# Value products of the segments' last tokens: one block of 32 tokens at each segment border, in place of a batched stage

## The chip, the core and the metric

The kernel runs on one core of a Trainium2 chip. The core has a matrix engine (PE, with its weight loads shown apart as PEld), a vector engine (DVE), a scalar engine (ACT), a general engine (POOL, which also issues DMAs) and a queue engine (SP, which issues most DMAs). The metric is the device time of one execution in microseconds. Before the change it is 3259.57 us, the median of three runs that lie between 3258.48 and 3265.56 us.

## What is computed

Four layers run one after the other, A B A B, on 2048 tokens of 640 values. Layers A hold nine tenths of the time. A layer A goes through 64 segments of 32 tokens, and each segment needs the one before it: the first 8 rows of a segment's result are the memory that stands ahead of the next segment's 32 tokens.

```python
for s in range(n_seg):
    h = concat([mem, x[:, 32*s : 32*s+32]])          # 8 + 32 rows
    q, k, v = h @ Wq, h @ Wk, h @ Wv                 # 32 heads of 192
    p = softmax(mask(q @ k.T * scale))
    o = (p @ v) @ Wo
    mem = o[:8]                                      # for the next segment
    outs.append(o[8:])
```

Of the 40 rows of `h`, 32 depend on `mem` or stand with it in one block (the 8 memory rows and the first 24 tokens). The last 8 tokens of each segment depend on no other segment in their q, k and v. Those eight are "the segment's last tokens" from here on. Layer B is a linear attention over all tokens, and the change does not touch it.

## The kernel before

**Stages.** The program runs, in each of the two layers A, first a batched stage (`A_pre`), which makes q, k and v of the last tokens of all 64 segments, and then the chain (`A_chain`), which goes through the segments in order. In the profiled execution the first layer's batched stage runs from the start to about 171 us and its chain to about 1370 us; the second layer's batched stage runs from 1643 to 1804 us and its chain to about 3000 us. The two layers B lie behind the two chains.

**The batched stage.** It has 8 steps: two halves of 32 segments by four rounds of 8 heads. A step makes K and Q of its 256 tokens (line 960, 120 matmuls), then V (line 989, 40 matmuls of 128x384). PSUM banks are emptied by DVE and ACT in turn (lines 97 and 99). K and Q go to DRAM as `kqb` (line 974), V goes to DRAM as `vb` (line 997, 64 DMAs of 97 KB a layer, issued by POOL). In the first layer the empty places between these copies are also used for the layer norm of all rows (`all_rows`: POOL loads a block of rows and stores the normalized block), and SP copies the output weights Wo from DRAM to DRAM into another order (`lay_out_wo`, line 792, all four rounds). `early_wo` and `late_wo` bring Wo into SBUF (line 751).

**The chain.** A segment has four rounds n = 0 to 3 of 8 heads each. Per round PE makes Q, K and V of the 32 rows (line 1092, 20 matmuls of 128x384 each, in four column groups of 32), then scores (line 1129), and P times V (line 1142); the products with Wo follow as filling between them (line 1198). ACT brings each PSUM bank to SBUF (lines 1107, 1119, 1172), DVE transposes it (lines 1112, 1285, 1293) or copies half of V (line 1121). For the last tokens POOL loads `kqb` (line 1062) and `vb` (`extra_v`, line 1073: 16 rows of 1552 bytes into rows 64 to 79 of `Vp`) and copies K and Q into place (line 1069).

**The border between two segments.** After the last product with Wo, DVE transposes the result (line 1371) and adds its two halves into the first 8 columns of `hT` (line 1373); PE can then start Q of the next segment. The other 24 columns of `hT` come from the next segment's own tokens: POOL loads them into the tile `xr` (`load_rows`, line 1040), and DVE transposes `xr` into `hT` (`hx_transpose`, line 1043) just ahead of the reciprocals of round 3 (line 1166). `load_rows` is called at the end of a segment for the segment after the next, so that the load has a whole segment's time before it is read. While DVE works at the border, PE runs four idle products of 128x512 (`keep_busy`, line 1205). ACT then copies half of the result (line 1051) and a tail (line 1183); DVE writes the rows to be stored into `orow` (line 1054), and POOL stores them (line 1058).

**Order.** In the chain the order on every engine is written out by hand: each engine goes through its instructions in the order of the program, and a waiting instruction holds up all behind it. SP streams seven pieces of 384 KB of Wq, Wk, Wv and four of 320 KB of Wo in each segment (lines 725 and 774); each is released by a matmul of the round. Each DMA of SP also waits until the eighth DMA before it has landed.

Of the kernel before, what the change touches and what calls it, by code (L numbers as in the profile page):

```python
# [8 lines left out]
P = 128  # L9
# [116 lines left out]
class Kernel:  # L126
# [114 lines left out]
    def rows_of(self, s):  # L241
        return self.xn_rows[32 * s:32 * s + 32, :].rearrange("t (q f) -> q t f", q=4)

# [435 lines left out]
    def layer_A(self, xn_dram, at_dram, li, x_raw=None):  # L679
# [6 lines left out]
        self.vb_d = dram.tile([NSEG, NR, 2, 8, 4 * VH], BF16, name=f"vb{li}")  # L686
# [55 lines left out]
        def load_wo(r, part):  # L742
            for k in part:
# [7 lines left out]
                nc.sync.dma_start(out=into, in_=self.wo_rows[r, :, 1280 * k:1280 * k + 1280])  # L751
# [21 lines left out]
        def load_piece(into, r, c):  # L773
            self.last_load = nc.sync.dma_start(out=into[:, c:c + 1280], in_=self.wo_rows[r, :, own + c:own + c + 1280])
            return self.last_load
# [10 lines left out]
        if li == 0:  # L786
            self.wo_rows = dram.tile([4, P, 7680], BF16, name="wo_rows")

        def lay_out_wo(r):
            for h in range(4):  # L790
                for G in range(2):
                    nc.sync.dma_start(out=self.wo_rows[r, 32 * h:32 * h + 32, 3840 * G:3840 * G + 3840]
                                      .rearrange("f (j m) -> f j m", m=640), in_=wov[8 * r + 4 * G + h])
# [17 lines left out]
    def A_pre(self, xn_dram, li, load_matrix, piece, wo_mid, wo_end, lay_out_wo, early_wo, x_raw):  # L811
# [11 lines left out]
        vts = [wo_end[:, 8 * VH * i:8 * VH * i + 8 * VH].rearrange("p (g f) -> p g f", f=2 * VH) for i in range(2)]  # L823
        with ExitStack() as es:
# [73 lines left out]
            def all_rows():  # L898
# [4 lines left out]
                return [f for i in range(0, len(t), 2) for f in (*t[i:i + 2], None)]  # L903

            for vt in vts:
                nc.vector.memset(vt, 1.0)
            if x_raw is not None:
                first = [norm_tasks(lambda x, k=k: gather(x, x_raw, 0, k, (nc.sync, nc.scalar)),
                                    lambda xn, k=k: normed.__setitem__((0, k), xn)) for k in range(NT)]
                for step in zip(*first):  # L910
                    for f in step:
                        f()
                warm = ps_.tile([P, 512], F32, name="ps_warm", tag="bank")

                def busy(n):
                    for _ in range(n):
                        nc.tensor.matmul(warm[:, :], lhsT=self.ident[:, :], rhs=vts[0].rearrange("p g f -> p (g f)")[:, 0:512],
# [3 lines left out]
            turn = nv = 0  # L921
# [5 lines left out]
            for h, ri, r in steps:  # L927
# [20 lines left out]
                if x_raw is not None and (h, ri) == (NH - 1, 0):  # L948
                    tasks += all_rows()
                if x_raw is not None and h == NH - 1 and ri == NR - 1:  # L950
# [17 lines left out]
                load_matrix("V", r)  # L968
# [6 lines left out]
                if x_raw is not None:  # L975
# [3 lines left out]
                    if h == NH - 1 and ri in (1, 2):  # L979
                        for r1 in (2 * ri - 2, 2 * ri - 1):  # L980
                            lay_out_wo(r1)
                w = [piece("V", r, b) for b in range(KC)]
                for k in range(NT):
                    vt = vts[nv % 2]
                    nv += 1
                    for g in range(4):
                        ps = ps_.tile([P, 512], F32, name="ps_pre", tag="bank")
                        for b in range(KC):
                            nc.tensor.matmul(ps[:, 0:384], lhsT=xBT[:, b, P * k:P * k + P],  # L989
                                             rhs=w[b][:, 384 * g:384 * g + 384], start=(b == 0), stop=(b == KC - 1))  # L990
                        evict(out=self.two_heads(vt[:, g, :]), in_=ps[:, 0:384].rearrange("p (e f) -> p e f", e=2))
                    if x_raw is not None and (h, ri, k) == (0, 0, 0):
# [3 lines left out]
                    for t2 in range(TP):  # L996
                        nc.gpsimd.dma_start(out=self.vb_d[SH * h:SH * h + SH, r, :, TP * k + t2, :],
                                            in_=vt[SH * t2:SH * t2 + SH, :, :].rearrange("p (g x) f -> p g (x f)", x=2))
# [4 lines left out]
    def A_chain(self, xn_dram, at_dram, li, load_slot, piece, late_wo, load_both, wo, low):  # L1003
# [3 lines left out]
        with tc.tile_pool(name=f"A{li}_ch", reuse_waits="tile", bufs=1) as sp, \  # L1007
# [9 lines left out]
            xr = sp.tile([P, 160], BF16, name="xr")  # L1017
            orow = self.under[:, self.ot_at + 768:self.ot_at + 928]
            nc.vector.memset(xr[:], 0.0)
            ots = [self.under[:, self.ot_at + 384 * i:self.ot_at + 384 * i + 384] for i in range(2)]  # L1020
            hT = sp.tile([P, KC, 32], BF16, name="hT", tag="hT")
# [17 lines left out]
            def load_rows(s):  # L1039
                nc.gpsimd.dma_start(out=xr[:], in_=self.rows_of(s))  # L1040

            def hx_transpose(hT, xr=xr):
                nc.vector.transpose(out=hT[:], in_=xr[:].rearrange("p (j b) -> p b j", b=KC))
# [27 lines left out]
            def extra_v(s, n):  # L1071
                r = rounds(s)[n]
                nc.gpsimd.dma_start(out=Vs[n % 2][64:80, :], in_=self.vb_d[s, r].rearrange("g t f -> (g t) f"))  # L1073
# [129 lines left out]
            def keep_busy(ps, w):  # L1203

                nc.tensor.matmul(ps[0:32, 0:w], lhsT=self.ident[:, 0:32], rhs=wo[1, 0][:, 0:w], start=True, stop=True,
                                 tile_position=(0, 0), skip_group_check=True)

# [5 lines left out]
            def weigh(E_before=None):  # L1213
# [5 lines left out]
                return E  # L1219

# [21 lines left out]
            for s in range(NSEG):  # L1242
# [18 lines left out]
                if s > 0:  # L1261
# [40 lines left out]
                for n in range(L):  # L1302
# [36 lines left out]
                    turn(n, osc)  # L1339
                    v_rows(pv, n + 1, "sv")  # L1340
# [128 lines left out]
```

## Time and profile before

| | |
|---|---|
| median of the runs shown | 3259.57 us |
| span of the profiled execution | 3253.7 us |
| PE busy | 3095.3 us, 95% of the span |
| DVE, ACT, POOL busy | 2208.8, 1883.0, 1410.7 us |
| batched stage, first layer (0 to 172 us) | PE 166.3 us busy, DMA share 0.93 |
| batched stage, second layer (1643 to 1810 us) | PE 163.8 us busy, DMA share 0.69 |
| a segment of the chain, border to border | median 18.39 us, mean 18.53 us, 124 of them |
| granted TensorE clock | 1.00 in both stages' windows and in the chain |

The profile is of one execution. Its span is 5.9 us under the median of the runs; no other time is given for the profiled execution, and what lies around its span is taken to be that difference. A group of instructions is shown with the tile that it writes, the tiles that it reads, its count, its busy time, the mean time of one, and the idle time of its engine just before it. Matmuls overlap in the array, so 20 of them with a mean of 0.33 us take 1.0 us together, and the busy time is what to add up.

### The profile page before, as it was taken

The numbers are of one execution on the slowest core, as the hardware profiler recorded it, in microseconds if no ns is written. First come the engines' busy times: TensorE is split into PE (matmuls) and PEld (weight loads), VectorE is DVE, ScalarE is ACT, GpSimd is POOL, SyncE is SP. The second block draws the span as 40 slices with busy tenths as digits, with TensorE's granted clock in tenths as the row PEclk, the third lists the DMA queues.
The fourth block names the chain that finished last, engine by engine and source line by source line (L and its number), as shares of the span: only waits on it lengthen the run. The fifth ranks groups of instructions, "written<-read, shape, count | busy, mean of one in ns | idle before, by whom it ended". The sixth has DMA issues, their size and how long they took to land.

```text
span 3253.7 us, 140890 instructions
## 1 busy us (share of the span) xinstructions
PE 3095.3 (95%) x59424; PEld 1980.2 (61%) x59730; DVE 2208.8 (68%) x5457; ACT 1883.0 (58%) x4481; POOL 1410.7 (43%) x2920
## 2 busy tenths in 40 slices
PE   9989999999999999999999899999999999999999
PEld 7756666666666666555367566666666666665553
DVE  5557777777777777666643577777777777776465
ACT  3346666666666666646433466666666666666453
POOL 3345555555455455430122355555555554554300
PEclk9999999999999999999999999999999999999999
DMA  8977777777777777840385677777777777778400
GB/s 306 372 271 253 256 248 257 232 255 253 236 256 245 244 257 238 285 166 1 113 319 193 240 233 257 248 252 256 242 264 240 259 244 245 255 236 282 149 1 33
DMA packets 325018, 747.58 MB, mean 230 GB/s; under 512 B 65818, under 2 KB 100274, under 8 KB 321314
## 3 DMA queue, kind: packets, MB, share of 16 engines
q1 hardware_dynamic: 254850, 638.55, 56.1%
q0 software_dynamic: 67616, 86.77, 9.7%
q10 hardware_dynamic: 1920, 13.24, 1.0%
q8 instruction: 469, 7.68, 1.0%
q14 instruction: 163, 1.34, 0.1%
HBM read 668.80 MB, written 77.03 MB: 229 GB/s over the span
## 4 chain that ended last, share of the span: by engine, by line
PE 75%; DMA 11%; DVE 8%; issue 3%; ACT 3%; POOL 0%; SPq 0%; PEld 0%; DVEq 0%; POOLq 0%; ACTq 0%
PE ps_qk_q L1092 12%; PE ps_qk_k L1092 12%; PE ps_v L1092 11%; PE ps_w L1198 10%; DMA arena<-in_A_Wv_dram 6%; PE ps_pre L960 6%; PE ps_s L1129 5%; PE ps_o L1142 3%; PE ps_pre L989 3%; PE kv L1424 2%; DVE raws L1371 2%; PE ps_wo L444 2%; DMA Vp<-vb 2%; DMA arena<-wo_rows 2%; DVE hT L1373 2%
## 5 line engine op out<-in xcount | busy, mean ns | idle before, releaser
L1092 PEld LDWEIGHTS <-hT 128*32 128x32 bf16 x30720 | 792.6, 97 | 422.7 <-issue 43.0
L1112 DVE STREAM_TRANSPOSE QK<-raws 128x512 bf16<-128x512 bf16 (+1 forms) x1152 | 730.7, 643 | 207.3 <-ACT raws L1107 166.7
L1092 PE MATMUL ps_qk_q<-arena,hT 128*32 128x384 bf16 x10240 | 510.4, 327 | 38.2 <-DVE hT L1373 31.1
L1069 POOL COPY QK<-kqb 64x192 bf16<-64x192 bf16 x1024 | 350.4, 342 | 380.9 <-PE ps_s L1129 344.3
L1092 PE MATMUL ps_qk_k<-arena,hT 128*32 128x384 bf16 x10240 | 511.7, 328 | 3.1 <-issue 1.2
L1107 ACT ACTIVATE raws<-ps_qk_k 128x512 bf16<-128x512 f32 (+1 forms) x640 | 313.5, 510 | 253.1 <-PE ps_qk_k L1092 253.1
L1092 PE MATMUL ps_v<-arena,hT 128*32 128x384 bf16 x8192 | 435.2, 326 | 15.2 <-DMA arena<-in_A_Wv_dram 7.2
L1073 POOL DMA_DIRECT2D Vp<-vb x512 | 257.6, 503 | 416.3 <-PE ps_t L1155 252.0
L1172 ACT ACTIVATE raws<-ps_o,rc 128x192 bf16<-128x192 f32 x1024 | 373.4, 420 | 109.3 <-DVE rc L1166 104.8
L1107 ACT ACTIVATE raws<-ps_qk_q 128x512 bf16<-128x512 f32 x512 | 305.7, 597 | 164.5 <-PE ps_qk_q L1092 153.4
L1198 PE MATMUL ps_w<-arena,under 128*32 128x320 bf16 x6144 | 307.4, 300 | 16.7 <-issue 13.1
L1062 POOL DMA_DIRECT2D kqb<-kqb x512 | 290.6, 568 | 70.2 <-POOL QK L1069 50.2
L1121 DVE CAST Vp<-ps_v 64x384 bf16<-64x384 f32 x512 | 286.4, 559 | 37.9 <-ACT Vp L1119 22.8
L1129 PEld LDWEIGHTS <-QK 128*80 128x80 bf16 x4096 | 195.8, 121 | 161.4 <-issue 157.3
L1119 ACT ACTIVATE Vp<-ps_v 64x384 bf16<-64x384 f32 x512 | 246.4, 481 | 55.5 <-PE ps_v L1092 54.2
L1129 PE MATMUL ps_s<-QK 128*80 128x80 bf16 x4096 | 256.8, 210 | 5.4 <-POOL QK L1069 2.8
L1218 ACT ACTIVATE E<-ps_s 80x320 bf16<-80x320 f32 x512 | 217.6, 425 | 32.3 <-PE ps_t L1155 28.9
L1051 ACT ACTIVATE wh<-ps_w 64x160 f32<-64x160 f32 x256 | 76.6, 299 | 264.8 <-DVE raws L1371 254.9
L1058 POOL DMA_DIRECT2D attn<-under x128 | 91.6, 716 | 292.8 <-DVE under L1054 289.7
L960 PEld LDWEIGHTS <-arena 128*128 128x128 bf16 x1920 | 188.4, 98 | 32.4 <-DVE next_xT L97 4.6
L97 DVE CAST arena<-ps_pre 128x512 bf16<-128x512 f32 (+1 forms) x160 | 102.2, 646 | 143.5 <-PE ps_pre L960 96.4
L1142 PE MATMUL ps_o<-Vp,E 80*32 80x193 bf16 x4096 | 180.3, 248 | 13.2 <-DMA Vp<-vb 3.7
(159 smaller groups left out, 4586.2 us busy)
## 6 DMA issues: line engine op xcount, KB each, us to landing
arena<-wo_rows SPq DMA_DIRECT2D x560, 320.0 KB, 5.6
arena<-in_A_Wq_dram SPq DMA_DIRECT2D x427, 384.0 KB, 4.3
arena<-in_A_Wk_dram SPq DMA_DIRECT2D x298, 384.0 KB, 4.8
arena<-in_A_Wv_dram SPq DMA_DIRECT2D x290, 384.0 KB, 6.0
kqb<-kqb POOLq DMA_DIRECT2D x512, 48.0 KB, 4.9
vb<-arena POOLq DMA_DIRECT2D x128, 97.0 KB, 6.1
Vp<-vb POOLq DMA_DIRECT2D x512, 24.2 KB, 4.0
kqb<-arena SPq DMA_DIRECT2D x8, 1536.0 KB, 10.0
```

The costliest lines, as they stand in the source:

```text
L960: nc.tensor.matmul(ps[:, T * i:T * i + T], lhsT=w[b][:, P * c:P * c + P], rhs=xBT[:, b, :], start=(b == 0), stop=(b == KC - 1))
L1062: nc.gpsimd.dma_start(out=kqb[:], in_=self.kqb_d[r, :, s, :])
L1069: nc.gpsimd.tensor_copy(out=o, in_=kqb[h, :].rearrange("p (x c q) -> p x c q", c=3, q=16))
L1073: nc.gpsimd.dma_start(out=Vs[n % 2][64:80, :], in_=self.vb_d[s, r].rearrange("g t f -> (g t) f"))
L1092: last = nc.tensor.matmul(o, lhsT=hT[:, b, :], rhs=rhs, start=(i == 0), stop=(i == KC - 1), tile_position=(0, 32 * g), skip_group_check=True)
L1107: nc.scalar.activation(out=raw[:, c], in_=ps[:, c], func=ACT.Copy)
L1112: nc.vector.transpose(out=o, in_=i)
L1121: nc.vector.tensor_copy(out=o, in_=i)
L1129: nc.tensor.matmul(S[0:80, c0:c0 + 80], lhsT=KT[:, 4 * x + c, :], rhs=QT[:, 4 * x + c, :], start=(c % 2 == 0), stop=(c % 2 == 1), skip_gro ...
L1142: nc.tensor.matmul(O[G][32 * h:32 * h + 32, VH * G:VH * G + 193], lhsT=E[0:80, 80 * h + 32 * G:80 * h + 32 * G + 32], rhs=V[0:80, VH * h:V ...
L1172: nc.scalar.activation(out=out, in_=i, func=ACT.Copy, scale=rc[G])
L1198: step = nc.tensor.matmul(W[q:q + 32, 0:320], lhsT=OT[i // 6][:, i % 6 // 2, 32 * (i % 2):32 * (i % 2) + 32], rhs=rhs, start=(first and i ...
```

## The change

V of the last tokens is no longer made in the batched stage, but for five blocks. A block is 32 tokens (the last 8 of each of 4 segments, a "set") by one round of 8 heads. There are 16 sets by 4 rounds, 64 blocks in a layer. `first_values` makes five of them in the batched stage (set 0, and round 0 of set 1); the others are made one at a border (`next_values`), where the four idle products stood: 20 matmuls into a PSUM bank of their own. Which block it is, `set_of(s)` says; it takes a round whose Wv is in SBUF at that border.

At the start of the next segment ACT copies the bank into `ots[0]` (`keep_values`, ahead of its copy of Q), and SP stores it in four DMAs of 24 KB (`store_values`). `ots[0]` is written again by DVE in round 0. Every fourth segment SP gathers the 32 tokens of the next set in four DMAs (`load_tails`, into a part of `ots[1]`), and DVE transposes them in round 0 (`turn_tails`). `vb` in DRAM has a new layout, so that `extra_v` reads 64 runs of 384 bytes in place of 16 of 1552.

To make room, `xr` has no tile of its own any more: it lies in the same bytes as `orow`. So the rows of the next segment are loaded within the segment before it, in round 1, after the store of `orow`. The batched stage also lays out only rounds 0 and 3 of Wo in DRAM; rounds 1 and 2 are loaded from Wo itself, in four DMAs of 80 KB for each one of 320 KB. V of round 0 and 3 is loaded less often in the second layer's batched stage.

```diff
+    def tail_values(self, ps, turned, r, piece):
+        for i in range(self.KC):
+            w = piece("V", r, i)
+            for g in range(4):
+                self.nc.tensor.matmul(ps[32 * g:32 * g + 32, 0:384], lhsT=turned[:, i, :], rhs=w[:, 384 * g:384 * g + 384],
...
+    def store_values(self, vt, k, r):
+        for p in range(4):
+            at = 384 * (p % 2)
+            self.nc.sync.dma_start(out=self.vb_d[k, r, :, p // 2, :, at:at + 384], in_=vt[32 * p:32 * p + 32, :])
...
-                        for r1 in (2 * ri - 2, 2 * ri - 1):
-                            lay_out_wo(r1)
-                w = [piece("V", r, b) for b in range(KC)]
-                for k in range(NT):
...
-                            nc.tensor.matmul(ps[:, 0:384], lhsT=xBT[:, b, P * k:P * k + P],
...
+                        lay_out_wo(3 * (ri - 1))
...
+                if h == NH - 1 and ri == 1:
+                    first_values(0, (3, 2))
...
+                if h == NH - 1 and ri == NR - 1:
+                    first_values(0, (1, 0))
+                    first_values(1, (0,))
...
-            xr = sp.tile([P, 160], BF16, name="xr")
-            orow = self.under[:, self.ot_at + 768:self.ot_at + 928]
+            orow = xr = self.under[:, self.ot_at + 768:self.ot_at + 928]
...
+            def set_of(s):
+                return (s + (4, 3, 2, 5)[s % 4]) // 4, (3, 1, 2, 0)[s % 4]
...
+            def keep_values():
+                if waiting:
+                    nc.scalar.activation(out=ots[0], in_=waiting[0][0][:, 0:384], func=ACT.Copy)
...
                     store_tail(otb, s - 1, rounds(s - 1)[L])
+                    keep_values()
+                load_tails(s)
                 turn_rows(q_or_k("Q", 0))
+                store_waiting()
...
                     turn(n, osc)
+                    if n == 0:
+                        turn_tails(s)
+                    if n == 1 and s > 0 and s + 1 < NSEG:
+                        load_rows(s + 1)
                     v_rows(pv, n + 1, "sv")
...
-                if s + 1 < NSEG:
-                    if s + 2 < NSEG:
-                        load_rows(s + 2)
                 wo_round(W, order[L], OTs[L], False, True, (*range(6, 12), *range(6)))
-                idle = pop.tile([P, 512], F32, name="ps_idle", tag="s")
-                for _ in range(4):
-                    keep_busy(idle, 512)
+                next_values(s)
                 fill(SEG_FILL)
```

More of the change, by code (lines that the diff above doesn't have):

```diff
@@ L786, in layer_A @@
         if li == 0:
[L787 removed]
+            self.wo_rows = dram.tile([2, P, 7680], BF16, name="wo_rows")
         def lay_out_wo(r):
@@ L822, in A_pre @@
         sts = [wo_mid[:, 6144 * i:6144 * i + 192 * SH].rearrange("p (s f) -> p s f", f=192) for i in range(2)]
-        vts = [wo_end[:, 8 * VH * i:8 * VH * i + 8 * VH].rearrange("p (g f) -> p g f", f=2 * VH) for i in range(2)]
+        vts = wo_end[:, 0:1920]
         with ExitStack() as es:
@@ L949, in A_pre @@
                     tasks += all_rows()
+                if (h, ri) == (NH - 1, 1):
+                    for k in range(2):
+                        self.gather_tails(nc.gpsimd, self.tails_place(k), k)
                 if x_raw is not None and h == NH - 1 and ri == NR - 1:
```

93 lines of the change are left out of this document (64 added, 29 removed).

## Prediction

> **What bounds the kernel now.** First the head of the page, then the busy time by stage, then one border of the chain engine by engine, last the time from a DMA's issue to its landing. The page:
>
> ```profile
> span 3253.7 us, 140890 instructions
> PE 3095.3 (95%) x59424; PEld 1980.2 (61%) x59730; DVE 2208.8 (68%) x5457; ACT 1883.0 (58%) x4481; POOL 1410.7 (43%) x2920
> ```
>
> PE is busy nearly everywhere, but idle products count as busy too, so the stages must be looked at one by one. Busy times in the two batched stages, all instructions first, then those of line 989 (V of the last tokens) alone; the columns are window, length, PE, PEld and, in the first fence, the other engines, then clock, DMA share, GB/s:
>
> ```profile
> 0.00:172.00 172.00, 166.32 (x1338) 129.43 (x1362) 92.74 (x236) 56.36 (x124) 58.99 (x131) 1.00 0.93 343
> 1643.00:1803.00 160.00, 158.66 (x1289) 126.54 (x1290) 54.13 (x90) 50.77 (x85) 40.31 (x77) 0.99 0.70 257
> ```
>
> ```profile
> 0.00:172.00 172.00, 53.47 (x320) 31.27 (x320) 1.00 0.93 343
> 1643.00:1810.00 167.00, 53.30 (x320) 31.31 (x320) 0.99 0.69 251
> ```
>
> PE bounds both stages, and V of the last tokens is 53.4 us of each. In the first the DMA engines are nearly full as well (0.93); in the second they are not (0.70).
>
> One segment of the chain (704.5 to 723.1 us), in four windows of the same columns:
>
> ```profile
> 704.50:709.50 5.00, 4.99 (x124) 3.34 (x128) 3.86 (x8) 3.36 (x8) 1.97 (x4) 1.00 0.72 214
> 709.50:714.50 5.00, 5.00 (x136) 3.32 (x128) 3.64 (x9) 3.71 (x10) 2.62 (x6) 1.00 0.95 343
> 714.50:719.50 5.00, 4.81 (x108) 2.69 (x100) 4.11 (x11) 3.62 (x10) 2.26 (x6) 1.00 0.92 327
> 719.50:723.10 3.60, 3.32 (x72) 2.02 (x69) 1.99 (x8) 1.07 (x4) 2.64 (x6) 1.00 0.24 53
> ```
>
> The DMA engines are full in the middle ten microseconds (0.95, 0.92) and almost idle at the border (0.24). Where in the segment a DMA is issued therefore decides how long it takes. Below, times with a plus count from the moment when hT is ready (end of the second addition, line 1373; 704.46 here); medians are over the 124 undisturbed segments of the trace, each 18.39 us.
>
> **The change part by part.**
>
> *Batched stages.* Removed on PE: 53.4 us a layer. Added: five blocks of 20 matmuls; the same 20 in the chain take 1.0 us, so 5 us. PE could gain 48 us a layer; the copies of these banks go with them and are no bound (DVE 93 us of 172). First layer: what the DMA engines move fills 0.93 x 172 = 160 us. Out of it go 62 DMAs of 97 KB of `vb` (6.2 MB, 17 us at 343/0.93 = 369 GB/s) and half of Wo's new layout (16 DMAs of 240 KB, 3.9 MB, 11 us); 0.5 MB of new stores (1 us) come in. That leaves 133 us, 140 at the share of 0.95 that the chain reaches, against 171 - 48 = 123 for PE: DMA is late next, and the gain is 31 us, not 48 (bounds 15, if the order of the loads leaves holes, and 48). Second layer: DMA needs 0.70 x 160 - 17 + 1 = 96 us, PE 112; the weights come at its beginning (share 1.00 from 1650 to 1690), so I take 40 of the 48 us (bounds 25 and 48). Together **-71 us** (-96 to -40).
>
> *First segment of each chain.* 24 DMAs of 80 KB replace six of 320 KB of Wo rounds 1 and 2, at most eight under way; by the 5.6 us that a piece of Wo takes to land, three times 5.6 = 17 us stand against some 6 + 6. This segment already waits for Wo. **+10 us** for both layers (0 to 20).
>
> *PE at the border.* Four idle products go, 20 matmuls like those of V come:
>
> ```profile
> L1092 PE MATMUL ps_v<-arena,hT 128*32 128x384 bf16 x8192 | 435.2, 326 | 15.2 <-DMA arena<-in_A_Wv_dram 7.2 <-issue 7.0
> L1205 PE MATMUL ps_idle<-arena,ident 128*32 128x512 bf16 x512 | 132.3, 381 | 0.0
> ```
>
> 20 x 435.2/8192 = 1.06 us against 4 x 132.3/512 = 1.03 us, both beside DVE's transposition and additions (ready 1.2 us after the products with Wo). **0**; uncovered, all of it would be 126 x 1.06 = 134 us, but nothing moves the cover away.
>
> *ACT at the border.*
>
> ```profile
> 704.09 0.61 ACT L1051 ACTIVATE wh<-ps_w 64x160 f32<-64x160 f32 x2 [1.82 <-DVE raws L1371]
> 704.72 0.42 ACT L1183 ACTIVATE otr<-ps_t,rct 128x192 bf16<-128x192 f32 x1
> 705.62 0.60 ACT L1107 ACTIVATE raws<-ps_qk_q 128x512 bf16<-128x512 f32 x1 [0.47 <-PE ps_qk_q L1092]
> ```
>
> The new copy of 128x384 (0.49 us, by the ACT copies of that shape in the batched stage) goes into the 0.47 us of idle time ahead of Q's copy. Behind it wait Q's copy, DVE's transposition and the scores. It overruns by some 0.05 us: **+6 us** (0 to 12).
>
> *Stores and gathers on SP.* Four stores are issued once ACT is done, at about +1.3, 0.33 us each by SP's other issues. Queued behind are the second and third load of Wq, then issued at about +2.6 and +3.0 in place of +1.42 and +2.56; they land by +7 to +7.5, and Q of round 3 starts at +9.5. DVE's write of `ots[0]` (line 1285, +6.16) waits for the stores; POOL's store of 48 KB issued at +1.94 lands at +5.86 (nine in ten by +6.51), so by that row it is in time. **0**, with 0.3 x 126 = 38 us as the far end. The gather and its transposition (0.34 us on DVE) come every fourth segment, where DVE soon idles 0.68 us (before line 1162): 0. `extra_v` moves the same 24 KB in shorter runs; `kqb`, of 384-byte runs and twice the bytes, takes 2.2 us where `Vp` takes 2.3: 0.
>
> *The rows of the next segment.* This is the part that counts. The load, issued at the border before (+16.7) and read 16 us later, is now issued in the same segment that reads it, in round 1. POOL, and then DVE where the rows are read:
>
> ```profile
> 713.64 0.50 POOL L1073 DMA_DIRECT2D Vp<-vb  x1 [1.26 <-PE ps_v L1092]
> 714.13 0.57 POOL L1062 DMA_DIRECT2D kqb<-kqb  x1
> 715.42 0.74 POOL L1069 COPY QK<-kqb 64x192 bf16<-64x192 bf16 x2 [0.71 <-PE ps_s L1129]
> ```
>
> ```profile
> 718.84 0.56 DVE L1121 CAST Vp<-ps_v 64x384 bf16<-64x384 f32 x1 [0.58 <-ACT Vp L1119]
> 719.32 0.34 DVE L1043 STREAM_TRANSPOSE hT<-xr 128x160 bf16<-128x160 bf16 x1
> 719.94 0.25 DVE L1166 RECIPROCAL rc<-ps_o 128x1 f32<-128x1 f32 x2 [0.28 <-PE ps_o L1142]
> ```
>
> The new issue stands right behind `kqb`, at +10.27; its 0.72 us fit into POOL's idle 0.71. On DVE the transposition can begin at +14.67 at the latest without pushing the reciprocals (+15.03). The load thus has 4.4 us. What loads of POOL take there, and at the border (KB each, us from issue to landing; windows 713.5 to 714.8 and 720.9 to 722.4):
>
> ```profile
> kqb<-kqb POOLq DMA_DIRECT2D x1, 48.0 KB, 5.8
> ```
>
> ```profile
> kqb<-kqb POOLq DMA_DIRECT2D x1, 48.0 KB, 2.3
> xr<-xn POOLq DMA_DIRECT2D x1, 40.0 KB, 2.7
> ```
>
> Over all segments the `kqb` of +9.69 takes 5.47 us (least 3.81) and lands at +15.17, the one of +12.20 lands at +16.76. Between them, a load issued at +10.27 lands at about +15.5, 0.8 us too late. Segment by segment, with that landing against the last moment in the same segment, the delay has a mean of 0.81 us; if it landed with the `kqb` just ahead, 0.49; 1.2 us behind that one, as `xr` lands behind `kqb` at the border, 1.64. Queued behind on DVE are the reciprocals, ACT's scaling, the last transposition and PE's last 24 products with Wo, which follow in the trace with no slack (transposed at 720.66 to 721.0, products from 721.09), then the border. So 124 x 0.81 = **+100 us** (61 to 203). I take the interpolation, as it lies between two rows of the same queue and load. In return PE's waits for late Wo pieces (3.5 + 4.4 + 1.5 us by the groups of line 1198) are partly covered: **-6 us** (-9 to 0).
>
> A rule of the Trainium skill speaks against this term (DMA: Bandwidth & Descriptors, section "Queues, rings and completion order"): each DMA engine takes turns between its queues packet by packet, so that a short load on POOL's queue would not stand behind SP's backlog; by it the term would be near 0. The trace does not agree as far as `kqb` shows it (5.8 against 2.3 us).
>
> *Sum:* -71 + 10 + 0 + 6 + 0 + 100 - 6 = +39 us. The profiled span becomes 3253.7 + 39 = 3292.7; with the 5.9 us by which the median lies above the span, **3299 us**.
>
> **The rivals.** *A, the load lands in time.* If it takes what it takes at the border (2.7 to 2.9 us), it is there at +13.2 and DVE waits for nothing: -71 + 10 + 6 = -55, **3205 us**, faster. It decides from a landing within 4.4 us. Against it stand the 5.47 us of the neighbour and 3.81 as its least; for it, that no `xr` was ever issued at this place. The Trainium skill's rule named above would give this case. Chance 0.20. *B, it lands 1.2 us behind `kqb`,* as at the border, where both are issued the same 0.57 us apart: 124 x 1.64 = 203, **3402 us**. Against it: in the first segment of the first chain, with full DMA engines, `xr` took 6.59 us where the `kqb` before it took 6.12, 1.4 us later only because it was issued 0.9 later. Chance 0.10. *C, the stores land too late as well,* and DVE's write of `ots[0]` with the products behind it (line 1198, 0.35 us after) slips by 0.5 us in each segment: +63, **3362 us**. Chance 0.08.
>
> **How the numbers follow.** My forecast has 0.62; its own bounds (61 to 140 us of waiting, 96 to 50 us of gain) reach from 3230 to 3355. Some 0.2% (6.5 us) is what a measurement of this kernel can tell from no change. Of the 0.62, 0.05 lie below 3253 us, 0.06 within 6.5 us of the time before, 0.51 above. With A faster (0.20) and B and C slower (0.18): faster 0.25, the same 0.06, slower 0.69. The range of 8 in 10 goes from A's 3205 to 3375, beyond C.
>
> **What would show it.** Batched stages: Q of the first segment starts at about 140 us in place of 170.8, and the second stage lasts about 120 in place of 160. Chain: DVE's transposition into hT has idle time ahead of it, ended by the DMA of the rows, of about 0.9 us in 124 segments, and a segment's median is 19.2 us in place of 18.39. Wrong if that wait is missing (A), if the segments grow with no wait there, or if the first stage's gain goes into stalls for weights.

## The result, and the profile after

The changed kernel takes **3483.77 us** (median of four runs, 3475.69 to 3491.40) against 3259.75 for the kernel before on the same chip: a ratio of 1.068, with an interval of 1.0655 to 1.0701. It is slower by 224 us, where 39 were forecast; the range ended at 3375. From here on, line numbers of the changed kernel are its own (Q, K and V in line 1130, the transposition into `hT` in 1080, the stores of the new values in 266).

The head of its page, span first, then busy time by engine:

```profile
span 3474.0 us, 145242 instructions
...
PE 3047.1 (88%) x60832; PEld 1953.1 (56%) x61138; DVE 2183.5 (63%) x5427; ACT 1909.7 (55%) x4540; POOL 1356.9 (39%) x2808
```

PE is busy for 48 us less than before (3095.3) and yet the span is 220 us longer, so the whole loss is idle time of PE, 268 us more of it. The two batched stages (columns as before: window, length, PE, PEld, DVE, ACT, POOL, clock, DMA share, GB/s):

```profile
0.00:142.00 142.00, 119.97 (x1106) 100.64 (x1110) 75.88 (x204) 44.98 (x93) 31.69 (x80) 0.98 0.91 334
1756.00:1882.00 126.00, 115.16 (x1074) 97.75 (x1078) 38.56 (x65) 36.92 (x59) 6.55 (x12) 0.97 0.74 281
```

Both are shorter, much as forecast. In the first PE is now idle for 22 of 142 us, with the DMA share at 0.91: 9.4 us ahead of its first products of all (2.6 before), 6.8 ahead of the products of the first blocks, whose tokens DVE has to transpose, and 3.0 for late Wk. The loss is in the chain. One segment of it (border at 707.1 us) in four windows of the same columns:

```profile
707.10:712.10 5.00, 4.99 (x124) 3.34 (x128) 3.86 (x8) 3.74 (x9) 1.98 (x4) 1.00 0.55 130
712.10:717.10 5.00, 5.00 (x136) 3.33 (x128) 3.63 (x9) 3.71 (x10) 2.60 (x6) 1.00 0.96 347
717.10:722.10 5.00, 4.11 (x96) 2.46 (x92) 3.56 (x10) 3.19 (x9) 2.74 (x6) 1.00 1.05 365
722.10:727.20 5.10, 3.75 (x104) 2.32 (x97) 2.65 (x9) 1.54 (x5) 2.23 (x5) 1.00 0.38 105
```

PE keeps up for ten microseconds and falls behind in the last ten (4.11 of 5.00, 3.75 of 5.10). The DMA share in the first window has dropped from 0.72 to 0.55, with 130 GB/s in place of 214: the loads of that window are later, and what they didn't move is still being moved in the third window and in the last. Two groups of waits grew in the chain, of PE for Wv and of DVE for the rows (us in total, times, longest; the first line is a group with its idle time ahead of it):

```profile
L1130 PE MATMUL ps_v<-arena,hT 128*32 128x384 bf16 x8192 | 454.2, 328 | 94.0 <-DMA arena<-in_A_Wv_dram 79.3
```

```profile
DVE hT L1080 <- DMA under<-xn: 136.7, 119, 3.0
```

Before, V had 15.2 us of idle time ahead of it, 7.2 of them for Wv, and the transposition none.

Where the 220 us come from, by moments of the two traces (first Q of a chain, each border, end of the span):

| part of the span, both layers together | before | after | difference | forecast |
|---|---|---|---|---|
| batched stages (with the first chain's last segment and layer B ahead of the second) | 620.0 us | 555.5 us | -64.5 | -71 |
| first segment of each chain | 64.9 | 99.7 | +34.8 | +10 |
| from the first to the last border of each chain, 62 segments, 124 in all | 2297.5 | 2546.4 | +248.9 | +100 |
| behind the last border of the second chain | 271.3 | 272.3 | +1.1 | 0 |

The forecast's terms of +6 for ACT and -6 for the waits for Wo, both in the third row, cancel.

The 124 segments of the third row are the "further segments" from here on. Their median went from 18.39 to 20.45 us, their mean from 18.53 to 20.54.

### The profile page after: what moved, and what is told of

Its sections match the earlier page's. It is cut to its first block, busy times and chain, and to the rows that moved or that the text cites. A ratio compares the mean times of both kernels' runs of the same rounds, so it can differ in the third digit from the quotient of the medians.

```text
span 3474.0 us, 145242 instructions
## 1 busy us (share of the span) xinstructions
PE 3047.1 (88%) x60832; PEld 1953.1 (56%) x61138; DVE 2183.5 (63%) x5427; ACT 1909.7 (55%) x4540; POOL 1356.9 (39%) x2808
## 4 chain that ended last, share of the span: by engine, by line
PE 52%; DMA 30%; DVE 8%; POOL 4%; issue 3%; ACT 2%; SPq 1%; PEld 0%; POOLq 0%; DVEq 0%; ACTq 0%
DMA under<-xn 20%; PE ps_qk_q L1130 10%; PE ps_qk_k L1130 9%; PE ps_v L1130 7%; PE ps_w L1236 6%; DMA arena<-in_A_Wv_dram 4%; PE ps_s L1167 3%; PE ps_pre L1003 2%; PE kv L1489 2%; DMA arena<-wo_rows 2%; DVE raws L1436 2%; POOL kqb L1099 2%; POOL Vp L1110 2%; PE ps_wo L468 2%; DVE hT L1438 1%
## 5 line engine op out<-in xcount | busy, mean ns | idle before, releaser
L1130 PEld LDWEIGHTS <-hT 128*32 128x32 bf16 x30720 | 810.1, 97 | 578.8 <-issue 196.1
L1130 PE MATMUL ps_qk_k<-arena,hT 128*32 128x384 bf16 x10240 | 530.2, 331 | 27.4 <-DMA arena<-in_A_Wk_dram 20.5
L1130 PE MATMUL ps_v<-arena,hT 128*32 128x384 bf16 x8192 | 454.2, 328 | 94.0 <-DMA arena<-in_A_Wv_dram 79.3
L1110 POOL DMA_DIRECT2D Vp<-vb x512 | 267.2, 522 | 653.0 <-PE ps_t L1193 383.0
L1236 PE MATMUL ps_w<-arena,QK 128*32 128x320 bf16 x3072 | 135.6, 305 | 122.9 <-DVE QK L1359 118.6
```

Of the source, the lines that this page charges most:

```text
L1110: nc.gpsimd.dma_start(out=Vs[n % 2][64:80, :].rearrange("p (q f) -> p q f", f=VH)[:, :, 0:192], in_=self.vb_d[s // 4, r, s % 4].rearrange( ...
L1130: last = nc.tensor.matmul(o, lhsT=hT[:, b, :], rhs=rhs, start=(i == 0), stop=(i == KC - 1), tile_position=(0, 32 * g), skip_group_check=True)
L1236: step = nc.tensor.matmul(W[q:q + 32, 0:320], lhsT=OT[i // 6][:, i % 6 // 2, 32 * (i % 2):32 * (i % 2) + 32], rhs=rhs, start=(first and i ...
```

## The experiments

Two suspects were left by these two traces. **Theory 1:** the rows of the next segment, issued in round 1, land too late, and by more than was forecast. **Theory 2:** the four stores hold SP, the weight loads queued behind them start late, and V of round 3 waits for Wv. The rival to both is the work at the border itself (products, copy, transposition). SP around the border at 707.1 us of the changed kernel (start, length, count; one line is a run of issues):

```profile
707.50 0.33 SPq L749 DMA_DIRECT2D arena<-in_A_Wq_dram  x1
708.15 2.50 SPq L266 DMA_DIRECT2D vb<-under  x4
710.75 1.01 SPq L749 DMA_DIRECT2D arena<-in_A_Wq_dram  x2
711.85 0.86 SPq L749 DMA_DIRECT2D arena<-in_A_Wk_dram  x2
712.85 0.82 SPq L749 DMA_DIRECT2D arena<-in_A_Wv_dram  x2
```

and of the kernel before, border at 704.5:

```profile
704.90 2.44 SPq L725 DMA_DIRECT2D arena<-in_A_Wq_dram  x3
707.99 1.68 SPq L725 DMA_DIRECT2D arena<-in_A_Wk_dram  x2
```

The stores take 2.50 us, not 4 x 0.33, and the second load of Wq starts 3.7 us behind the border in place of 1.4.

Each table row below gives the median time, its ratio to the kernel before with its interval, and the differences of one profile from that of before, in the parts of the table above. One profile is one execution: in e10 and e5 its two chains, which do the same work, differ by 11 and 15 us.

| kernel | us | ratio | stages | first segments | further segments |
|---|---|---|---|---|---|
| changed | 3483.8 | 1.068 [1.066, 1.070] | -64 | +35 | +249 |
| e1_rows_early | 3380.5 | 1.035 [1.031, 1.039] | -60 | +33 | +155 |
| e4_before_rows_late | 3435.4 | 1.052 [1.047, 1.057] | -1 | -1 | +173 |
| e10_before_four_stores | 3382.4 | 1.037 [1.035, 1.038] | +1 | -1 | +126 |
| e12_before_both | 3497.2 | 1.072 [1.069, 1.076] | +1 | -1 | +242 |
| e11_before_one_store | 3278.4 | 1.005 [1.003, 1.007] | +3 | -2 | +29 |
| e13_before_four_short | 3348.6 | 1.026 [1.022, 1.030] | -2 | -1 | +97 |
| e14_before_four_tiny | 3360.8 | 1.031 [1.029, 1.034] | +1 | -2 | +106 |
| e15_before_stores_late | 3261.7 | 1.000 [0.999, 1.002] | +2 | -1 | +9 |
| e6_one_store | 3401.2 | 1.042 [1.039, 1.045] | -64 | +24 | +187 |
| e9_four_stores_short | 3465.8 | 1.062 [1.059, 1.065] | -66 | +28 | +245 |
| e2_stores_on_pool | 3752.1 | 1.149 [1.146, 1.153] | -59 | +32 | +532 |
| e3_both | 3643.2 | 1.116 [1.111, 1.121] | -63 | +35 | +421 |
| e5_wo_laid_out | 3476.6 | 1.065 [1.061, 1.069] | -56 | +13 | +268 |
| e8_rows_plain | 3368.9 | 1.033 [1.028, 1.037] | -5 | -1 | +119 |
| e7_store_rows_wo | 3240.3 | 0.993 [0.990, 0.995] | -62 | +5 | +37 |

### The rows: e1 takes the late load out of the change, e4 puts it alone into the kernel before

e1, the changed kernel with the rows' own tile and the load back at the border:

```diff
-            orow = xr = self.under[:, self.ot_at + 768:self.ot_at + 928]
+            xr = sp.tile([P, 160], BF16, name="xr")[:]
+            orow = self.under[:, self.ot_at + 768:self.ot_at + 928]
...
-                    if n == 1 and s > 0 and s + 1 < NSEG:
-                        load_rows(s + 1)
...
+                if s + 2 < NSEG:
+                    load_rows(s + 2)
```

(The tile of the turned tokens is cut in two to make room, so DVE transposes them in two steps.)

> The changed kernel, but the rows of the next segment but one are loaded at the border again, into a tile of their own, as in the kernel before. Theory 1 (two separate costs in each segment: about 1.05 us of DVE's wait for the rows, and about 1.0 us of late weights because four stores hold up the queue engine): the wait of the transposition into hT is gone, the segment goes from 20.45 to about 19.4 us, the time from 3484 to about 3354 us. Rival 2 (the late weights alone carry the cost, and the wait for the rows only fills time that V of round 3 leaves idle anyway): the time stays within 20 us of 3484.

e4, the kernel before with the opposite edit:

> The kernel before with one part of the change alone: the rows of the next segment share the bytes of the rows to be stored and are loaded in round 1 of the segment that reads them. The prediction's term for this part was 0.81 us in each of 124 segments, +100 us, 3360 us. Theory 1 says the same order of size (0.8 to 1.05 us, 3360 to 3390 us), with a wait ahead of the transposition into hT that the DMA of the rows ends. If the wait of 1.05 us seen in the changed kernel comes from the late weights there (which delay the load of the rows behind them), it is nearer to 0.8 here.

e1 gains 103 us, less than the 130 expected, and still has 155 us of extra time in the further segments; there the wait for Wv stays (86.5 us). So the rows are one cause and not the only one. e4 shows the rows alone, and they cost more than its expectation had (3435 us against 3360 to 3390): the wait ahead of line 1041, e4's transposition, comes with every segment, 1.58 us each.

```profile
DVE hT L1041 <- DMA under<-xn: 196.5, 124, 3.5
```

In e4 the load is issued at +10.28 and lands at +16.12 in the median, 0.77 us behind the `kqb` issued just before it (+15.35) and 0.95 ahead of the next one (+17.07). The forecast had +15.5.

### The stores: e10 puts them alone into the kernel before, e11 to e15 vary them

e10, with a table that nothing reads:

```diff
                 turn_rows(q_or_k("Q", 0))
+                if s > 0:
+                    for p in range(4):
+                        nc.sync.dma_start(out=extra_d[s // 4, s % 4, :, p // 2, :, 384 * (p % 2):384 * (p % 2) + 384],
+                                          in_=ots[0][32 * p:32 * p + 32, :])
```

> The kernel before, and in each segment from the second on four stores on SP of the shape of the change's (32 x 384 of ots[0], the DRAM side 4 x 8 x 384) at the place of the change's stores, into a table that nothing reads. No product is added or moved, and the rows are loaded where before has them. Theory that SP's issue time is the price: four issues of 0.59 us push the Wq loads of rounds 2 and 3 and then Wk and Wv back by 1 to 2 us, PE waits for V of round 3, and a segment is 0.9 to 1.2 us longer: 3370 to 3415. Rival (the 1.25 us a segment that the changed kernel keeps with early rows is made by the products, casts and transpositions at the border): 3260 to 3290.

e11 stores all 128 rows in one DMA:

```diff
+                    nc.sync.dma_start(out=extra_d[s // 4, s % 4].rearrange("t (g f) -> g t f", g=4), in_=ots[0])
```

> The same with one store of all 128 rows in place of the four: the same bytes, one issue of 0.53 us. Theory of the issue time: the Wq loads stay at +1.7 and +2.6 us and Wv where it was, and the time is 3260 to 3275. Rival (the bytes or the rows of the stores hold the weights up on the DMA engines, not the issue on SP): as e10 within 15 us.

Both came out as theory 2 has it (e11 3 us above its range). Without a product or a late row, e10 is 119 us above before, and its V waits for Wv as in the changed kernel; e11, with the same bytes, hardly does. One link of e10's expectation is not so: the second and third load of Wq are issued 2.1 and 1.4 us later than before, but Wv goes out at +5.79 and +6.28 in the median, as before (0.2 us later in the mean). What is late is its landing, shown with e13 below. The group of V in e10, and the same in e11:

```profile
L1092 PE MATMUL ps_v<-arena,hT 128*32 128x384 bf16 x8192 | 452.9, 327 | 91.5 <-DMA arena<-in_A_Wv_dram 74.6 <-issue 16.1
```

```profile
L1092 PE MATMUL ps_v<-arena,hT 128*32 128x384 bf16 x8192 | 439.0, 327 | 22.2 <-DMA arena<-in_A_Wv_dram 11.5 <-issue 10.4
```

But four against one also changes the number of DMAs under way, of which SP has at most eight. Two runs on the changed kernel had left that open. e6 has one store a block, with the table's layout to suit; e9 has the same layout and four stores of a plain 32 x 384:

```diff
-        for p in range(4):
-            at = 384 * (p % 2)
-            self.nc.sync.dma_start(out=self.vb_d[k, r, :, p // 2, :, at:at + 384], in_=vt[32 * p:32 * p + 32, :])
+        for g in range(4):
+            self.nc.sync.dma_start(out=self.vb_d[k, r, :, 384 * g:384 * g + 384], in_=vt[32 * g:32 * g + 32, :])
```

> The changed kernel, but the values of a block go to DRAM in one DMA of 128 rows instead of four of 32 rows (the layout in DRAM and the order of the 16 rows of K and V are changed so that one read still fetches them). Same bytes, and by its shape also on few engines, but SP is held up once (0.6 to 0.7 us) instead of for 2.5 us. Theory 1 (SP's issue time makes the weights late): PE's waits for Wk and Wv fall from 0.79 us a segment to about 0.2, the wait for the rows stays 1.0 to 1.5 us, the segment is about 19.8 us as with the rows late alone, the time 3484 - 80 = about 3400 us. Rival (bytes or few engines make them late): 3484, unchanged.

> As with one store, same new layout in DRAM, but in four DMAs of 32 rows, each a plain two-dimensional one: SP should be held up about 0.33 us for each, 1.4 us together, and each can use all 16 engines. Theory 1 (SP's issue time): between the changed kernel and the one-store kernel, near the middle, about 3440 us. Rival (few engines): better than the one store, below 3400 us.

e6 came where it was expected, e9 did not: it holds SP for 1.78 us, and of 249 us it keeps 245. Its waits for Wv fell by half (79.3 to 41.3 us), but those for the rows rose from 136.7 to 164.8: the rows land at +16.72, hardly earlier than in the changed kernel (+16.77), and a shorter wait for V only lengthens the wait behind it. So the stores were varied where the rows are not late, in the kernel before. e13 has the short stores of e9, e14 the stores of e10 with 16 columns in place of 384, e15 the stores of e10 unchanged behind the segment's last load of Wo:

```diff
                 turn(L, oscs)
+                if s + 1 < NSEG:
+                    for p in range(4):
+                        nc.sync.dma_start(out=extra_d[s // 4, s % 4, :, p // 2, :, 384 * (p % 2):384 * (p % 2) + 384],
+                                          in_=ots[0][32 * p:32 * p + 32, :])
                 output_steps(len(outs))
```

> As e10, but the DRAM side of each of the four stores is a plain 32 x 384 block, so that an issue takes 0.41 us in place of 0.59 and SP is held 1.8 us in place of 2.5. The same four DMAs and the same bytes. If the price goes with the time that SP is held (3382 for 2.50 us, 3278 for 0.52, both above 3263): about 3345. If it goes with the number of DMAs (each takes one of the eight that SP may have under way): 3370 to 3390.

> As e10, but each of the four stores takes 16 columns in place of 384: the same four issues of the same form (about 0.59 us each), but 1 KB each in place of 24, so hardly any bytes. If the hold on SP or the number of DMAs is the price: 3365 to 3390, as e10. If the bytes are: 3265 to 3290.

> The four stores of e10 unchanged in form, number and bytes, but behind the segment's last load of Wo, at about +11.6 us, where SP then has nothing to issue until the next border. If the price is that loads of weights stand queued behind the stores: 3260 to 3290. If four stores a segment cost by their bytes or their places among the eight wherever they stand: 3350 to 3390.

| stores a segment | SP held | above before (3263.5 for e10 and e11, else 3259.0) |
|---|---|---|
| e11: one, 96 KB | 0.52 us | +15 us |
| e13: four of 24 KB, plain | 1.77 | +90 |
| e14: four of 1 KB | 2.51 | +102 |
| e10: four of 24 KB | 2.50 | +119 |
| e15: four of 24 KB, late | 2.50 | +3, not to be told from 0 |

The price follows the time for which SP is held in front of the weights. e14, 4 us below the range for that, leaves 17 us for the bytes. Four stores a segment are free where SP has nothing to issue behind them: neither the bytes nor the number of DMAs costs anything in e15. The limit of eight DMAs under way, which e15 alone would not exclude, did not bind in front of the weights either: in e13, where most landings on SP's queue can be read, the stores land at +4.2 to +5.8 in the median, and the eighth DMA behind each is issued at +5.8 to +9.1.

The landings of e13 also show how the weights become late. The second and third load of Wq land 1.0 and 1.5 us later than before (+6.83 and +8.36), those of Wk both 1.5 us (+9.70 and +11.18), and those of Wv, issued as before, 0.7 and 0.8 us (+12.22 and +13.33 in place of +11.49 and +12.55). SP in e15, with the stores in the idle time ahead of the next border's Wq:

```profile
700.83 2.50 SPq L1361 DMA_DIRECT2D extra<-under  x4
707.55 2.44 SPq L725 DMA_DIRECT2D arena<-in_A_Wq_dram  x3
```

### Both causes together: e12

e12 is the kernel before with the edits of e4 and e10.

> The kernel before with both causes and nothing else of the change: the rows loaded in round 1 (e4) and the four stores on SP (e10). Alone they cost 1.39 us and 0.98 us a segment by the profiles. Theory of the same slack: both make V and the rows of round 3 late, and the longer of the two covers part of the other, as in the changed kernel, where its further segments are 1.99 us longer in the mean and the products at the border are worth about 0.2 of it: 1.7 to 1.9 us a segment, 3475 to 3500. Rival (they simply add): 2.37 us a segment, 3550 to 3565. If the products and copies at the border carry more than the 0.2 us, it ends below 3470.

The further segments grow by 242 us, against 173 + 126 = 299 if the two simply added and 249 in the changed kernel. So these two edits alone give nearly all of what the chain lost, without one product moved, and they share slack. What is left for the products, the copy, the transposition and the gathers is 249 - 242 = 7 us, and 155 - 126 = 29 us by e1 against e10, where one profile's chains differ by 11 us and e1's stores, which wait for ACT's copy, start at +1.10 in place of +0.87: the rival had a small part at most.

How they share it can be read off the landing of the rows. Medians over the further segments:

| kernel | rows land at | next border at |
|---|---|---|
| e8 (below) | +15.72 | +19.34 |
| e4 | +16.12 | +19.72 |
| e6 | +16.33 | +19.95 |
| e9 | +16.72 | +20.39 |
| e12 | +16.73 | +20.36 |
| changed | +16.77 | +20.45 |

Wherever the rows are late, the next border follows their landing by 3.6 to 3.7 us, and DVE's cast of V (its copy of half of V) is over before they land (in 97% of the changed kernel's segments). There the stores lengthen a segment by making the rows land later, 16.73 against 16.12 in e12 and e4, and the wait for V ahead of them adds little; where the rows are early, as in e1 and e10, the wait for V shows by itself.

### The stores on POOL: e2, and with early rows e3

```diff
-                    self.store_values(ots[0], k, r)
+                    self.store_values(ots[0], k, r, nc.gpsimd)
```

> The changed kernel, but the four stores of the values at each border are issued by POOL in place of SP; same bytes, same places. Theory 1 (SP is held up for 2.5 us by the four stores, so that the weight loads behind them start late): Wq's second load of a segment is issued at about +1.4 us again in place of +3.7, PE's waits for Wk and Wv (20 and 79 us) nearly vanish, the segment goes to about 19.4 us and the time to about 3360 us. Rival 3 (the DMA engines themselves carry too much, with short runs and stores that use few engines): the weights come as late as before, the time stays at 3484 or rises, as POOL has more to issue.

> Both edits at once: rows loaded at the border into their own tile, and stores issued by POOL. Theory 1: the segment is back at about 18.45 us; with 64 us gained in the batched stages and 35 us lost in the two first segments the time is about 3230 to 3240 us, below the kernel before. Rival 3: the segment stays at 19.4 us, the time at 3354.

Both missed by far: 3752 us against about 3360 expected, and 3643 against 3230 to 3240. Issuing on POOL frees SP, and PE's wait for Wv is gone (0.5 us in e2), but e2 is 268 us slower than the changed kernel:

```profile
DVE under L1351 <- DMA vb<-under: 423.0, 118, 5.3
```

DVE's write of `ots[0]` in round 0 now waits for the stores, 3.6 us in each of 118 segments. They are issued at +2.75 to +4.54 and land 4.7 to 5.2 us later, at +7.4 to +9.7, behind the write's +6.16. It is rival C's mechanism, at some seven times the 0.5 us that it was given, and only from this queue: from SP the stores are there in time. The two runs say nothing against theory 2; they trade its wait for a longer one.

### The loads of Wo: e5

e5 is the changed kernel with all four rounds of Wo laid out in DRAM, as before, and so without the 48 small loads around the first segment.

> The changed kernel, but all four rounds of Wo are laid out in DRAM and loaded in pieces of 320 KB again. The first segment of each chain takes 51.7 and 48 us in the changed kernel against 33.7 and 31 before, and SP spends 16.5 and 17.3 us on the 48 small loads of the first chain. Theory: the small loads hold up SP ahead of the stores of the first values and of Wo, so the first segments shrink by 12 to 17 us each, the first batched stage grows by up to 10 us with the copies, and the time goes from 3484 to about 3460 us (3445 to 3475). Rival: the first segments wait for the bytes, not for the issue; the time stays within 8 us of 3484.

In its profile the first segments cost 22 us less than in the changed kernel and the batched stages 8 us more (more of Wo is laid out there). Its second chain was 18 us longer than the changed kernel's in that execution for no reason found, and the medians differ by 7 us only, with spreads that overlap: the time is where the rival had it. The first segments' share is shown; what e5 gains in all is not.

What lengthens a first segment is shown by the changed kernel's first chain: first PE, then SP.

```profile
158.38 1.09 PE L1167 MATMUL ps_s<-QK 128*80 128x80 bf16 x8 [10.23 <-POOL QK L1106]
...
179.59 0.32 PE L1236 MATMUL ps_w<-arena,under 128*32 128x320 bf16 x4 [2.04 <-DMA arena<-in_A_Wo_dram]
```

```profile
130.95 16.49 SPq L780 DMA_DIRECT2D arena<-in_A_Wo_dram  x24
...
148.01 9.18 SPq L266 DMA_DIRECT2D vb<-arena  x12
```

The small loads hold SP for 16.5 us, then come the stores of the first blocks for 9.2 us, and POOL, which reads those blocks back and then copies K and Q, waits 20 us for them; the first scores stand 10.2 us (2.67 before).

### The shape of the rows' load: e8

e8 is e4 with the rows read as a plain block; it leaves out the order of a token's quarters, so its values are not the kernel's.

```diff
-                nc.gpsimd.dma_start(out=xr, in_=self.rows_of(s))
+                nc.gpsimd.dma_start(out=xr, in_=self.xn_rows[32 * s:32 * s + 32, :].rearrange("t (q f) -> (t q) f", q=4))
```

> The kernel before with the rows loaded in round 1 as in e4, but each 32-token block is read as a plain 128 x 160 block of memory (one run of 320 bytes a row of the tile, in the order of the memory) where the kernel has a token's four quarters on four groups of 32 rows. It leaves that order out: the layers then compute with a token's parts in other places, so the values are not the kernel's. Shape theory (the rows land behind kqb of 12.09 because their packets run over fewer DMA engines at a time): the latency of the rows falls from 5.8 us to that of kqb, 5.0 to 5.5, they land 0.5 us earlier, the DVE wait of 1.58 us a segment falls to about 1.0, and e4's 3435 falls by some 70 us to about 3365. Backlog theory (the bytes of the weights ahead of them alone set the time): latency stays at 5.7 to 6.0 and the time at 3425 to 3445.

The same 40 KB land 5.42 us behind the start of their issue in place of 5.79, at +15.72 in place of +16.12, and the time falls by 66 us. So a part of the price of the late rows is the shape of their DMA, not only the load on the engines. Of the 0.37 us, 0.16 are the issue itself, which takes POOL 0.55 us in place of 0.71. The Trainium skill (DMA: Bandwidth & Descriptors, section "Why a DMA increments its semaphore by 16 and not by 1") lets the slowest dimensions of the two sides decide over how many engines a DMA is spread: with 4 quarters on the DRAM side that would be 4 engines, with 128 rows 16. The earlier landing agrees with that as far as the other 0.2 us go; over how many engines either load ran, the traces do not tell.

### A version that beats both: e7

e7 is the changed kernel with one store a block (e6), the rows loaded at the border (e1) and all of Wo laid out (e5).

> The changed kernel with the three costs undone at once: one store, the rows loaded early into a tile of their own, Wo laid out as before. What stays is that V of the last tokens is made at the borders. If the three are all that the change costs: the segment is back at 18.4 to 18.6 us, the batched stages keep 55 to 64 us of gain, and the time is 3195 to 3215 us, faster than the kernel before (3260). If making the values in the chain has a cost of its own (ACT's copy, POOL's shorter runs, DMA bytes), the segment is 18.8 us or more and the time 3235 us or more.

At 3240.25 us it is 0.7% faster than the kernel before, where 3195 to 3215 was expected if only the three costs counted. The stages keep -62 us and the first segments cost 5, but the further ones still cost 37, of which one store alone is 29 by e11. In its profile V waits for Wv for 6.8 us in all (7.2 before), and DVE has no idle time ahead of the transposition into `hT`:

```profile
L1075 DVE STREAM_TRANSPOSE hT<-xr 128x160 bf16<-128x160 bf16 x126 | 43.7, 347 | 0.0
```

## Why the prediction was wrong, step by step

- *Batched stages, -71:* right in size. Q of the first segment starts at 141.6 us ("about 140") and the second stage is 35 us shorter (40 taken); together -64. The reason given for the first stage, that the DMA engines bound it at 140 us, is not shown: of PE's 22 idle us only 3.0 end with a weight load, so how near it came may be luck.
- *First segment, +10 (0 to 20):* too small; it is +35. Only Wo was counted, worth about 22 by e5, and of its 48 small loads only the 24 inside the first segment; the other 24 hold SP for 16.5 us just ahead of it. The stores of the first blocks on SP, and POOL's wait for them, were not counted.
- *PE at the border, 0:* right. The 20 products take the place of the idle ones; e12 has none of the new products and loses 242 of 249 us.
- *ACT at the border, +6:* nothing of it is seen. The copy takes the idle time, and Q's copy follows with no gap, at +1.16 us behind the border as before:

```profile
707.64 0.48 ACT L1277 ACTIVATE under<-ps_x 128x384 bf16<-128x384 f32 x1
708.22 0.60 ACT L1145 ACTIVATE raws<-ps_qk_q 128x512 bf16<-128x512 f32 x1
```

- *Stores and gathers on SP, 0 (38 at the far end):* **the step that failed first.** It is +126 us alone. Two things were wrong in it. The issue was priced "by SP's other issues" at 0.33 us, but those are loads of 128 plain rows; a store with a DRAM side of 4 x 8 x 384 takes 0.59. And the loads queued behind were followed to the next reader only, Q of round 3, which they do reach in time. Behind the Wq loads stand Wk and Wv, for which the DMA engines were already full (share 0.95): in e13 Wv is issued when it was before and lands 0.7 and 0.8 us later. The first microseconds behind the border, with a lower DMA share (0.72), were no free time: there the stream got its lead, and with the stores the share falls to 0.55.
- *The rows, +100 (61 to 203):* the mechanism was right, the size was not: +173 alone, near rival B's 203. The moment of the landing is what failed, +15.5 in the forecast and +16.12 in e4. "Between two rows of the same queue and load" was sound for the place and wrong for the DMA: both rows are `kqb`, and e8 shows that another shape lands earlier. In the changed kernel the pushed-back weights are added, and the rows land at +16.77, 6.47 us after their issue (6.2 in the segment shown below). By the prediction's own sum that is 16.77 - 14.67 = 2.10 us too late; the median of a segment grew by 2.06.

```profile
kqb<-kqb POOLq DMA_DIRECT2D x1, 48.0 KB, 6.0
under<-xn POOLq DMA_DIRECT2D x1, 40.0 KB, 6.2
```

DVE then stands still once for V and once for the rows, ahead of line 1080 (start, length; idle time and what ended it in brackets):

```profile
721.99 0.56 DVE L1159 CAST Vp<-ps_v 64x384 bf16<-64x384 f32 x1 [1.14 <-ACT Vp L1157]
723.60 0.37 DVE L1080 STREAM_TRANSPOSE hT<-under 128x160 bf16<-128x160 bf16 x1 [1.05 <-DMA under<-xn]
724.00 0.23 DVE L1204 RECIPROCAL rc<-ps_o 128x1 f32<-128x1 f32 x2
```

The wait for the rows is 1.10 us in the mean, close to the "about 0.9" that was to show the step; but a segment is 20.45 us in place of the 19.2 forecast. The wait for V stands in front and hides part of the rows' delay: the landing, not the length of that one wait, says how late they are. Reading the wait alone would have passed the step as right.
- *Wo's waits, -6:* too small to matter. Outside the two first segments they are nearly gone.
- *Rival A* (the rows in time) did not happen: their load took 5.8 to 6.5 us beside SP's stream against 2.9 at the idle border. So what the prediction drew from the Trainium skill's rule on turns between queues (DMA: Bandwidth & Descriptors, section "Queues, rings and completion order"), a term near 0, did not come true here. *Rival C* did not happen with the stores on SP.

In short, the forecast had the direction right, by way of a real cost, but two of its terms failed: the stores on SP, put at 0, and the rows, put to land at +15.5. Together they make 242 of the 249 us (e12).

What stays open: whether e5 gains anything in all, how the rows' 5.4 us in a plain shape divide between the stream's backlog and anything else, and why some issues of Wk take over 0.8 us behind the stores (in 34 of 124 segments of e10, in 5 before), and Wv is issued 0.2 us later in the mean.

## What to carry to other kernels

When an instruction is put into a queue that streams at its limit, follow everything behind it to the end of the stream, not only the first reader: 2.5 us at the head of SP's queue cost 0.8 to 1.0 us in each segment, and nothing where the queue was empty. Take the duration of a DMA's issue and of its landing from a row of the same shape, or bound it by the worst shape in the trace. And when two late arrivals share one slack, undo them one at a time and put them in one at a time: 173 and 126 us alone gave 242 together.

## What was not expected of the hardware

- In these runs the time that SP takes to issue one DMA goes with the form of its access and not with its bytes: 0.33 us for 384 KB as 128 plain rows (some 0.4 right behind another issue), 0.41 for 32 x 384, 0.53 for 128 rows against a three-dimensional DRAM side, 0.59 for 32 rows against 4 x 8 x 384, and as long for the same form with 1 KB (four in 2.51 us).
- A store of 24 KB at the border lands 3.2 to 3.4 us after its issue from SP in e13 and 4.7 to 5.2 us after its issue from POOL in e2. The two also differ in the DRAM side (32 x 384 and 4 x 8 x 384) and in the moment (1.9 to 2.3 us later in e2), so the queue is not shown to be the cause.
- In e2, where DVE's wait of 3.6 us a segment holds PE up, the mean granted clock is 0.936 and a matmul of V has a mean of 346 ns; in e10 they are 0.990 and 327 ns.
